# Retention and a swish layer on one core: first weights by half rows, ups in pairs of column groups, no copy of chunk 3's scores

## The chip, the cores and the metric

The kernel runs on one core of one Trainium2 chip. The metric is device time in microseconds (us): the median of three runs before the change is 311.66 us (311.6 to 312.2). The engines are named as the profile names them: PE (TensorE; PEld is its weight load), DVE (VectorE), ACT (ScalarE), POOL (GpSimd) and SP (SyncE, which here only issues DMAs).

## The reference

Eight batches with eight heads of 576 positions and 64 columns go through retention (scores times a decay that depends on the head and the distance, causal, without a softmax). The heads' outputs side by side are the 512 columns of 4608 tokens, and these go through a layer with a swish between its two products:

```python
scores = scale * np.matmul(q, k.transpose(0, 1, 3, 2))
gamma = 1.0 - 2.0 ** (-5.0 - np.arange(H, dtype=np.float32))
rel = pos[:, None] - pos[None, :]
Dmat = np.where(rel >= 0, gamma[:, None, None] ** rel[None, :, :], 0.0)
attn = np.matmul(scores * Dmat[None, :, :, :], v)
x = attn.transpose(0, 2, 1, 3).reshape(B * S, H * D)      # 4608 x 512
h = x @ w_in                                              # w_in 512 x 2048
g = h * (1.0 / (1.0 + np.exp(-beta * h)))                 # beta: 2048
out = g @ w_out                                           # w_out 2048 x 512
```

Inputs and output are float32.

## The kernel before

**Tiling.** The first 512 positions of each batch are a block of four chunks of 128; the last 64 of two batches make a tail chunk, and four tail chunks are the ninth block. Chunks are numbered in the order in which they are worked, so block 0 has chunks 0 to 3 and block 1 chunks 4 to 7. The decay is a factor on q (`gq`) and one on v (`gv`), so what stays of it in the scores is a mask of zeros and ones.

**Retention of one chunk i.** `pre` makes kn (k as bf16) and vn (v times its factor) on POOL. `t_k` turns kn on PE into a PSUM tile T, and ACT copies it to kT; `t_q` does the same for q, for half of the heads at a time. `a_sc` makes the scores of the eight heads (8 matmuls into two PSUM banks, even heads and odd heads) and DVE multiplies each bank with the mask into R. `a_O` multiplies R with vn (8 matmuls into a bank O), `a_cross` adds what the state of the earlier chunks gives (4 matmuls), and `a_x` copies O to xT, the transposed input of the layer. `a_st` adds the chunk to the state (4 matmuls), and ACT copies it to sbd (or end) in two pieces. In block 0 `a_cross` comes ahead of `a_O`, in block 1 behind it.

**The layer of one block m.** `up` makes one of 16 column groups of h: 4 matmuls (ko 0 to 3, one for each 128 rows of w_in) of 512 columns, and one ACT activation to gT. `down` is a quarter of the sum for one of four output tiles (4 matmuls); after a tile's last quarter DVE copies it to ot, and SP issues its store.

**Weights.** w_in is loaded in pieces of columns, four of 256 and two of 512, each with one DMA for all four row groups, into four staging tiles of 512 columns; `cast_w_in` casts each row group to bf16 on DVE or POOL. w_out comes in four groups of four column groups through the same four staging buffers, so each of its loads waits for the casts of the w_in tile whose buffer it takes; `cast_w_out` scales three on DVE and one on ACT.

**Order.** Nothing is scheduled by a planner: each engine's instructions stand in the order in which the program emits them, and each engine works its own in that order. Up to line 502 the order is written out by hand. Then `fill`, a list of ups and downs, is emitted one by one, and each step of `streams` is emitted ahead of the first fill entry whose number is not below the step's number. d0 is the number of block 0's first down (16), u1 that of block 1's first up (d0 + 16). Block 0's downs go by quarters for tiles 0 to 2 (d0 to d0 + 11), then tile 3 (d0 + 12 to d0 + 15).

**PSUM.** The eight banks are shared by tag: `mm` has three (ups, downs, warm-up matmuls, the second half of t_q, the scores of chunk 3), `O` two (O, T, and the scores of odd chunks from 5 on), `sc` two (other scores, T of chunks 6 and 7), `st` one. An instruction that opens a tile waits until the last reader of the bank's former tile is done.

**Lines.** L81 load_q, L94 load_kv, L178 load_w_in, L186 cast_w_in, L190 load_w_out, L198 and L200 cast_w_out, L208 warm_up, L247 qs, L255 vn, L273 kn, L297 and L303 transposes, L298 and L304 their copies, L323 scores, L330 the copy of chunk 3's odd scores, L333 the mask product, L351 the cross product, L366 O, L380, L381 and L384 xT, L396 and L401 the state, L413 and L415 up, L426 and L433 down, L436 the store.

Of the kernel before, what the change touches and what calls it, by code (L numbers as in the profile page):

```python
# [11 lines left out]
F32 = mybir.dt.float32  # L12
BF16 = mybir.dt.bfloat16
ACT = mybir.ActivationFunctionType
ALU = mybir.AluOpType
# [4 lines left out]
def kernel(  # L20
# [110 lines left out]
    for h in range(H):  # L131
# [13 lines left out]
    nc.gpsimd.memset(causal[:], 1.0)  # L145
    nc.gpsimd.affine_select(out=causal[:], in_=causal[:], pattern=[[1, CB], [CB, PC]], compare_op=ALU.is_ge,
                            fill=0.0, base=0, channel_multiplier=-1)
    causal4 = consts.tile([P, HP, P], BF16, name="causal4")
    nc.gpsimd.tensor_copy(causal4[:], causal[:].unsqueeze(1).to_broadcast([P, HP, P]))

    causal2 = consts.tile([P, P], BF16, name="causal2")

    NS = 3
# [10 lines left out]
    tiny = consts.tile([P, FO], F32, name="tiny")  # L164
    WG = 4

    pieces = [(f, 256) for f in range(0, 1024, 256)] + [(f, 512) for f in range(1024, d_ff, 512)]
    NP = len(pieces)
    w_in_r = moe_w_in.rearrange("(ko ki) f -> ki ko f", ki=P)
    w_out_r = moe_w_out.rearrange("(fo fi) n -> fi fo n", fi=P)  # L170
# [2 lines left out]
    def load_w_in(g):  # L173
        f0, fn = pieces[g]
        if f0 % 512 == 0:
            whole[0] = stage.tile([P, KO, 512], F32, name="wt", tag="wt", bufs=4)
        t = whole[0][:, :, f0 % 512:f0 % 512 + fn]
        nc.sync.dma_start(t, w_in_r[:, :, f0:f0 + fn])  # L178
        wts[g] = t

    def cast_w_in(g, kos=range(KO)):
        t = wts[g]
        f0, fn = pieces[g]
        for ko in kos:
            on_pool = ko == KO - 1 or g < 4 and ko > 1
            (nc.gpsimd if on_pool else nc.vector).tensor_copy(w_in_sb[:, ko, f0:f0 + fn], t[:, ko])  # L186

    def load_w_out(g):
        t = stage.tile([P, KO, d_model], F32, name="wt", tag="wt", bufs=4)
# [15 lines left out]
    def warm_up(n, cols=256):  # L205
        ph = psum.tile([P, MB], F32, name="ph", tag="mm", bufs=3)
        for _ in range(n):
            nc.tensor.matmul(ph[:, :cols], warm[:, :P], warm[:, :cols], start=True, stop=True,  # L208
                             skip_group_check=True)
# [41 lines left out]
    def pre(i, js=(0, 1)):  # L251

        b, c = seq[i]
        if 0 not in js:
            nc.gpsimd.tensor_tensor(live[i]["vn"][:], kv_tiles.pop(i)[:, 1], gains(gv, c), ALU.mult)  # L255
            return
        vn = sb.tile([P, H, D], BF16, name="vn", tag="vn", bufs=6)
        if b is None:
            t = tail_tiles.pop(c)
            qk = sb.tile([P, 2, H, D], BF16, name="kn", tag="kn", bufs=4)  # L260
            qkT = sb.tile([P, 2, HP, P], BF16, name="kT", tag="kT", bufs=4)
            nc.gpsimd.tensor_tensor(qk[:, 0], t[:, 0], gains(gq, CB), ALU.mult)
            nc.gpsimd.tensor_copy(qk[:, 1], t[:, 1])
            nc.gpsimd.tensor_tensor(vn[:], t[:, 2], gains(gv, CB), ALU.mult)
            live[i] = dict(qk=qk, qkT=qkT, kT=qkT[:, 1], vn=vn)
            return
        if c % 2 == 0:
            pair[b, c // 2] = (sb.tile([P, 2, H, D], BF16, name="kn", tag="kn", bufs=4),
                               sb.tile([P, 2, HP, P], BF16, name="kT", tag="kT", bufs=4))
        t = kv_tiles[i]  # L270
        kn, kT = pair[b, c // 2]
        live[i] = dict(kn=kn[:, c % 2], kT=kT[:, c % 2], vn=vn)
        nc.gpsimd.tensor_copy(kn[:, c % 2], t[:, 0])  # L273
        if 1 in js:
            pre(i, (1,))
# [24 lines left out]
    def t_k(i):  # L300
        T = psum.tile([P, HP, P], BF16, name="T", tag="sc" if i in (CB + 2, CB + 3) else "O", bufs=2)
        for p in range(HP):
            nc.tensor.transpose(T[:, p, :], heads(live[i]["kn"], p), ident[:])  # L303
        nc.scalar.copy(live[i]["kT"], T[:])  # L304

    def q_cols(i, r, p):

# [5 lines left out]
    def a_sc(i):  # L313
        L = live[i]
        L["R"] = R = sb.tile([P, 2, HP, P], BF16, name="R", tag="R", bufs=4)

        tag = "mm" if i == CB - 1 else "O" if i >= E and (i - E) % 2 else "sc"
        sc = [psum.tile([P, HP, P], F32, name="sc", tag=tag, bufs=3 if tag == "mm" else 2) for _ in range(2)]
        for p in range(HP):
            for j in range(2):  # L320
                r = slice(j * D, (j + 1) * D)
                rhs, view = q_cols(i, r, p)
                nc.tensor.matmul(view(sc[j][:, p, :]), L["kT"][r, p, :], rhs, start=True, stop=True,  # L323
                                 skip_group_check=True)
        mask = causal if seq[i][0] is not None else causal2
        m_b = mask[:].unsqueeze(1).to_broadcast([P, HP, P])
        if i == CB - 1:

            half = sb.tile([P, HP, P], BF16, name="half", tag="half", bufs=1)
            nc.scalar.copy(half[:], sc[1][:])  # L330
            sc[1] = half
        for j in range(2):
            nc.vector.tensor_tensor(R[:, j], sc[j][:], causal4[:] if i == CB - 1 else m_b, ALU.mult)  # L333

    def a_cross(i, first):

# [17 lines left out]
    def a_O(i):  # L354

        b, c = seq[i]
        L = live[i]

        early = i < E
        if not early:  # L360
            tag = "sc" if b is not None and b >= QB and c > 1 else "O"
            L["O"] = psum.tile([P, HP, P], F32, name="O", tag=tag, bufs=2)
        O, R, vn = L["O"], L["R"], L["vn"]
        crossed = b is None or c > 0
        for j, p in [(n // HP, n % HP) if early else (n % 2, n // 2) for n in range(H)]:
            nc.tensor.matmul(O[j * D:(j + 1) * D, p, :], vn[:, 2 * p + j, :], R[:, j, p, :],  # L366
                             start=p == 0 and not (early and crossed), stop=early or not crossed,
                             skip_group_check=True)
        if early:
            a_x(i)  # L370

    def a_x(i):
        b, c = seq[i]
        O = live[i]["O"]
        if b is None:
            x = xt(B)[:, :, c, :]
        else:
            x, O = xt(b)[:, :, :, c * PC:(c + 1) * PC], O.rearrange("k p (i s) -> k p i s", i=CB)
        if i == CB - 1:
            nc.vector.tensor_copy(x[:, :2], O[:, :2])  # L380
            nc.scalar.copy(x[:, 2:], O[:, 2:])  # L381
        else:
            on_act = i < E or i % 2 == 0 if i < 2 * E else b is not None and c == 1
            (nc.scalar.copy if on_act else nc.vector.tensor_copy)(x, O[:])  # L384

    def a_st(i):
# [19 lines left out]
    def up(m, fo, c0=0, cn=CB):  # L406
        if m not in gts:
            gts[m] = sb.tile([P, FO, CB, P], BF16, name="gT", tag="gT", bufs=2)
        w = slice(c0 * PC, (c0 + cn) * PC)
        ph = psum.tile([P, CB, P], F32, name="ph", tag="mm", bufs=3)  # L410
        ph = ph.rearrange("f i s -> f (i s)")[:, :cn * P].rearrange("f (i s) -> f i s", i=CB)
        for ko in range(KO):
            nc.tensor.matmul(ph, w_in_sb[:, ko, fo * P:(fo + 1) * P], xts[m][:, ko, :, w],  # L413
                             start=(ko == 0), stop=(ko == KO - 1))
        nc.scalar.activation(gts[m][:, fo, :, w], ph, ACT.Silu, scale=beta_sb[:, fo:fo + 1])  # L415

    pos_, ots = {}, {}

# [34 lines left out]
    def F(f, *a):  # L453
        return lambda: f(*a)
# [17 lines left out]
    warm_up(1, 128)  # L472
    a_cross(0, True)
    a_O(0)
    a_sc(1)
    a_cross(1, True)
    pre(2, (0,))
# [3 lines left out]
    pre(3, (0,))  # L481
    a_sc(2)
    t_k(3)
    warm_up(1, 128)
    a_cross(2, True)
    a_sc(3)
    pre(2, (1,))
    a_st(2)
    a_O(2)
    pre(3, (1,))  # L490
    warm_up(2, 128)
    a_cross(3, True)
    a_O(3)
    cast_w_in(0)
    a_st(3)
    cast_w_in(1)
    nc.vector.reciprocal(rbeta_sb[:], beta_sb[:])

# [2 lines left out]
                            fill=0.0, base=0, channel_multiplier=-1)  # L501
    nc.gpsimd.memset(causal2[:TL, TL:], 0.0)

    fill = [F(up, 0, fo) for fo in range(FO)]
    d0 = len(fill)
    fill += [F(down, 0, ms, f0) for f0 in range(0, FO, 4) for ms in range(3)]
    fill += [F(down, 0, 3, f0) for f0 in range(0, FO, 4)]
# [13 lines left out]
    def second(i):  # L521
        for f in (a_O, lambda j: a_cross(j, False), a_x):
# [1 line left out]
            f(i + 1)  # L524
        a_st(i + 1)

    streams = [[(0, F(load_w_out, 0)), (1.1, F(cast_w_in, 2)), (3.1, F(cast_w_in, 3)), (3.2, F(load_w_out, 1)),
                (6.1, F(cast_w_in, 4)), (6.2, F(load_w_out, 2)), (10.1, F(cast_w_in, 5)), (10.2, F(load_w_out, 3))],
               [(d0 - 4 + 3.3 * g, F(cast_w_out, g)) for g in range(WG)],
               [(10.3, F(load_q, 1))] + [(10.3, F(load_kv, CB + n, (j,))) for n, j in keys_first],  # L530
               [(10.4, F(load_q, 2))] + [(10.4, F(load_kv, 2 * CB + n)) for n in range(2)],
               [(d0 + 8.6, F(load_kv, 2 * CB + 2)), (d0 + 10.1, F(load_kv, 2 * CB + 3))],
               [(d0 + 7, F(pre_q, 1, n)) for n in range(4)] + [(d0 + 10.6, F(t_q, 1, 0)), (d0 + 12.6, F(t_q, 1, 1))],
               [(d0 + 8, F(pre, 4, (0,))), (d0 + 8, F(pre, 5, (0,))), (d0 + 9, F(pre, 4, (1,))), (d0 + 9, F(pre, 5, (1,))),
                (d0 + 12.7, F(t_k, 4)), (d0 + 12.8, F(t_k, 5)), (d0 + 13.8, F(a_sc, 4)), (d0 + 13.81, F(a_sc, 5)),
                (d0 + 14.8, F(a_st, 4)), (d0 + 15.9, F(second, 4))],
               [(d0 + 10, F(pre, 6, (0,))), (d0 + 10, F(pre, 7, (0,))), (d0 + 12, F(pre, 6, (1,))), (d0 + 12, F(pre, 7, (1,))),
                (d0 + 15.8, F(t_k, 6)), (d0 + 15.91, F(t_k, 7)), (u1 + 1.8, F(a_sc, 6)), (u1 + 1.81, F(a_sc, 7)),
                (u1 + 2.8, F(a_st, 6)), (u1 + 8.8, F(second, 6))]]
# [81 lines left out]
```

## Time and profile before

| | us |
|---|---|
| median of three runs | 311.66 |
| the profiled execution | 311.92 |
| its span (first to last instruction) | 310.1 |
| PE busy | 298.5 (96%) |
| ACT busy | 143.0 (46%) |
| DVE busy | 106.9 (34%) |
| POOL busy | 96.0 (31%) |
| first up of block 0 | 19.48 |
| first down of block 0 | 34.28 |
| first up of block 1 | 52.22 |
| last matmul ends | 306.83 |

A row of the timeline gives start, length, engine, line, operation, the tile written and the tile read, and the count; in brackets stands how long the engine had been idle and what ended that. A row of the chain of waits gives start, length and the work that the end of the program goes back to. The granted clock of PE is 0.998 of the full one.

### The profile page before, as it was taken

Reading aid. Unit: us, or ns where it says so; the run is one execution under the profiler, and the core shown is the slowest. Engines: PE = TensorE matmul, PEld = TensorE weight load, DVE = VectorE, ACT = ScalarE, POOL = GpSimd, SP = SyncE. Lnnn points to the kernel's source line nnn. Section 1 sums busy time; section 2 is a strip of 40 time slices with the busy share of each in tenths; the row PEclk is TensorE's granted clock in tenths of the full one; section 3 lists DMA queues with packets and bytes.
Section 4 is the critical chain, followed back from the end, with each engine's and each line's share of the span. In section 5 each row is a group of like instructions: output and inputs, shape, how many; then the busy total and the mean of one; then the engine's idle time right before and its main releaser. Section 6 shows DMA issues by size and latency. Waiting matters only on the chain.

```text
span 310.1 us, 5363 instructions
## 1 busy us (share of the span) xinstructions
PE 298.5 (96%) x2144; PEld 157.8 (51%) x2177; DVE 106.9 (34%) x191; ACT 143.0 (46%) x256; POOL 96.0 (31%) x131
## 2 busy tenths in 40 slices
PE   7789999999999999999999999999999999999995
PEld 5544456775544454454554545455545444444444
DVE  7554476342531342434430434043405420010012
ACT  5567626995138412560186117711673037207700
POOL 4663026846524282254308031902420000000000
PEclk9999999999999999999999999999999999999999
DMA  8999999998989999999897697968852110031011
GB/s 207 221 355 387 380 232 273 233 257 179 202 197 162 224 189 235 218 212 198 133 234 107 136 205 207 201 115 192 196 76 37 68 70 0 17 88 34 0 70 68
DMA packets 123897, 52.79 MB, mean 170 GB/s; under 512 B 105680, under 2 KB 116320, under 8 KB 123872
## 3 DMA queue, kind: packets, MB, share of 16 engines
q1 hardware_dynamic: 98496, 46.15, 61.5%
q10 hardware_dynamic: 25376, 6.30, 13.6%
q8 instruction: 17, 0.28, 0.4%
q14 instruction: 8, 0.07, 0.1%
HBM read 36.71 MB, written 9.44 MB: 149 GB/s over the span
## 4 chain that ended last, share of the span: by engine, by line
PE 85%; DMA 6%; SPq 5%; DVE 1%; issue 1%; ACT 1%; POOL 1%; POOLq 0%
PE po L426 40%; PE ph L413 35%; DMA wt<-in_moe_w_in_dram 4%; SPq L94 3%; PE O L366 3%; PE sc L323 3%; DMA qn<-in_q_dram 2%; PE O L351 2%; PE st L396 2%; SPq L178 1%; POOL qs L247 1%; PE T L297 1%; PE T L303 1%; ACT gT L415 0%; DVE xT L384 0%
## 5 line engine op out<-in xcount | busy, mean ns | idle before, releaser
L415 ACT ACTIVATE gT<-ph,beta_sb 128x512 bf16<-128x512 f32 (+1 forms) x154 | 99.2, 659 | 86.3 <-PE ph L413 83.4
L413 PE MATMUL ph<-xT,w_in_sb 128*128 128x512 bf16 (+1 forms) x600 | 129.3, 365 | 3.2 <-DVE w_in_sb L186 0.9
L426 PE MATMUL po<-w_out_sb,gT 128*128 128x512 bf16 (+2 forms) x591 | 126.7, 368 | 1.1 <-issue 0.3
L413 PEld LDWEIGHTS <-w_in_sb 128*128 128x128 bf16 x616 | 58.7, 98 | 65.0 <-DVE w_in_sb L186 2.3
L426 PEld LDWEIGHTS <-gT 128*128 128x128 bf16 x608 | 57.1, 98 | 62.5
L333 DVE TENSOR_TENSOR R<-sc,causal 128x512 bf16<-128x512 f32 x71 | 44.3, 684 | 68.9 <-PE sc L323 68.9
L433 DVE COPY ot<-po 128x512 f32<-128x512 f32 (+2 forms) x38 | 25.0, 662 | 92.1 <-PE po L426 92.0
L255 POOL TENSOR_TENSOR vn<-kvn,gv 128x512 bf16<-128x512 f32 x32 | 33.4, 1042 | 22.8 <-DMA kvn<-in_v_dram 11.5
L247 POOL TENSOR_TENSOR qs<-qn,gq 128x512 bf16<-128x512 f32 x24 | 24.3, 1042 | 33.2 <-DMA qn<-in_q_dram 33.2
L273 POOL CAST kn<-kvn 128x512 bf16<-128x512 f32 x32 | 19.6, 612 | 47.7 <-DMA kvn<-in_k_dram 47.3
L401 ACT CAST sbd<-st 64x256 bf16<-64x256 f32 x48 | 17.4, 362 | 15.0 <-PE st L396 14.3
L384 DVE CAST xT<-O 128x512 bf16<-128x512 f32 x24 | 15.8, 688 | 19.6 <-PE O L366 9.6
L384 ACT CAST xT<-O 128x512 bf16<-128x512 f32 x11 | 6.4, 586 | 32.2 <-PE O L351 25.2
L396 PE MATMUL st<-vn,kn 128*128 128x128 bf16 x128 | 12.4, 219 | 0.2 <-POOL vn L255 0.2
L396 PEld LDWEIGHTS <-kn 128*128 128x128 bf16 x128 | 9.3, 98 | 5.0 <-issue 0.2
L366 PE MATMUL O<-R,vn 128*64 128x128 bf16 x288 | 10.7, 221 | 0.0
L323 PE MATMUL sc<-qT,kT 64*128 64x128 bf16 x256 | 10.3, 217 | 0.4 <-ACT kT L304 0.2
L366 PEld LDWEIGHTS <-vn 128*64 128x64 bf16 x288 | 8.5, 110 | 4.1 <-issue 3.6
L323 PEld LDWEIGHTS <-kT 64*128 64x128 bf16 x288 | 8.1, 94 | 3.8 <-ACT kT L304 1.5
L304 ACT COPY kT<-T 128x512 bf16<-128x512 bf16 x12 | 6.9, 586 | 4.8 <-PE T L303 4.8
L208 PE MATMUL ph<-warm 128*128 128x128 f32 (+1 forms) x24 | 7.0, 429 | 1.2 <-DVE warm L119 1.2
L186 DVE CAST w_in_sb<-wt 128x256 bf16<-128x256 f32 (+1 forms) x14 | 6.0, 476 | 5.2 <-DMA wt<-in_moe_w_in_dram 5.2
(56 smaller groups left out, 90.2 us busy)
## 6 DMA issues: line engine op xcount, KB each, us to landing
qn<-in_q_dram SPq DMA_DIRECT2D x16, 512.0 KB, 5.8
kvn<-in_k_dram SPq DMA_DIRECT2D x32, 256.0 KB, 5.9
kvn<-in_v_dram SPq DMA_DIRECT2D x32, 256.0 KB, 5.6
out_dram<-ot SPq DMA_DIRECT2D x31, 256.0 KB, 2.7
wt<-in_moe_w_out_dram SPq DMA_DIRECT2D x4, 1024.0 KB, 9.5
wt<-in_moe_w_in_dram SPq DMA_DIRECT2D x4, 512.0 KB, 7.5
wt<-in_moe_w_in_dram SPq DMA_DIRECT2D x2, 1024.0 KB, 11.8
out_dram<-ot SPq DMA_DIRECT2D x9, 128.0 KB, 2.4
```

The lines of the kernel that those rows point to most:

```text
L247: e.tensor_tensor(batch[b]["qs"][:, cs, hs], q_tiles[b][:, hs, cs].rearrange("p h i d -> p i h d"), gq[:, cs, hs].unsqueeze(3).to_broadcas ...
L255: nc.gpsimd.tensor_tensor(live[i]["vn"][:], kv_tiles.pop(i)[:, 1], gains(gv, c), ALU.mult)
L273: nc.gpsimd.tensor_copy(kn[:, c % 2], t[:, 0])
L323: nc.tensor.matmul(view(sc[j][:, p, :]), L["kT"][r, p, :], rhs, start=True, stop=True, skip_group_check=True)
L333: nc.vector.tensor_tensor(R[:, j], sc[j][:], causal4[:] if i == CB - 1 else m_b, ALU.mult)
L366: nc.tensor.matmul(O[j * D:(j + 1) * D, p, :], vn[:, 2 * p + j, :], R[:, j, p, :], start=p == 0 and not (early and crossed), stop=early or ...
L384: (nc.scalar.copy if on_act else nc.vector.tensor_copy)(x, O[:])
L396: nc.tensor.matmul(st[:, p, :], heads(L["kn"], p), heads(L["vn"], p), start=(c == 0 and p == 0), stop=True, skip_group_check=True)
L413: nc.tensor.matmul(ph, w_in_sb[:, ko, fo * P:(fo + 1) * P], xts[m][:, ko, :, w], start=(ko == 0), stop=(ko == KO - 1))
L415: nc.scalar.activation(gts[m][:, fo, :, w], ph, ACT.Silu, scale=beta_sb[:, fo:fo + 1])
L426: nc.tensor.matmul(po[:, :nn], gT[:, fo, ms, :], w_out_sb[:, fo, n0:n0 + nn], start=(fo == 0), stop=(fo == FO - 1))
L433: nc.vector.tensor_copy(ot, po[:, :nn])
```

## The change

- w_in is loaded in six pieces of 256 columns and one of 512, each by two DMAs, one for its first two row groups and one for the other two.
- `cast_w_in` gives even row groups to DVE and odd ones to POOL; of the first piece group 0 goes to POOL, 1 to ACT, 2 to DVE, 3 to POOL.
- Block 0's ups go in pairs of column groups: the matmuls of ko 0 and 1 for both, then those of ko 2 and 3 for both, each group's activation behind its own.
- Chunk 3's odd scores are multiplied with the mask straight from PSUM; the copy `half` and the widened mask `causal4` are gone.
- `a_x` of chunks 0 to 3 is called by itself, for chunk 1 behind the transposes of chunk 3's keys. xT of chunks 3, 5 and 7 is copied by halves, by DVE and ACT; of chunks 4 and 6 by ACT. kT of chunks 5 and 7 is copied by DVE.
- `a_st(3)` stands between the two halves of the first pair. Casts, loads of w_out and block 1's transposes, scores and chunk 4's state have other numbers in `streams`.

```diff
-    causal4 = consts.tile([P, HP, P], BF16, name="causal4")
-    nc.gpsimd.tensor_copy(causal4[:], causal[:].unsqueeze(1).to_broadcast([P, HP, P]))
...
-    pieces = [(f, 256) for f in range(0, 1024, 256)] + [(f, 512) for f in range(1024, d_ff, 512)]
+    pieces = [(f, 256) for f in range(0, 1536, 256)] + [(f, 512) for f in range(1536, d_ff, 512)]
...
         t = whole[0][:, :, f0 % 512:f0 % 512 + fn]
-        nc.sync.dma_start(t, w_in_r[:, :, f0:f0 + fn])
+        for u in range(2):
+            w = slice(u * KO // 2, (u + 1) * KO // 2)
+            nc.sync.dma_start(t[:, w], w_in_r[:, w, f0:f0 + fn])
...
         for ko in kos:
-            on_pool = ko == KO - 1 or g < 4 and ko > 1
-            (nc.gpsimd if on_pool else nc.vector).tensor_copy(w_in_sb[:, ko, f0:f0 + fn], t[:, ko])
+            if g == 0 and ko == 1:
+                nc.scalar.copy(w_in_sb[:, ko, f0:f0 + fn], t[:, ko])
+            else:
+                on_pool = ko == 0 if g == 0 and ko < 2 else ko % 2
+                (nc.gpsimd if on_pool else nc.vector).tensor_copy(w_in_sb[:, ko, f0:f0 + fn], t[:, ko])
...
-        nc.scalar.copy(live[i]["kT"], T[:])
+        (nc.vector.tensor_copy if i > CB and i % 2 else nc.scalar.copy)(live[i]["kT"], T[:])
...
-        if i == CB - 1:
-
-            half = sb.tile([P, HP, P], BF16, name="half", tag="half", bufs=1)
-            nc.scalar.copy(half[:], sc[1][:])
-            sc[1] = half
         for j in range(2):
-            nc.vector.tensor_tensor(R[:, j], sc[j][:], causal4[:] if i == CB - 1 else m_b, ALU.mult)
+            nc.vector.tensor_tensor(R[:, j], sc[j][:], m_b, ALU.mult)
...
-        if early:
-            a_x(i)
...
-        if i == CB - 1:
+        if i < 2 * CB and i % 2 and i != 1:
             nc.vector.tensor_copy(x[:, :2], O[:, :2])
             nc.scalar.copy(x[:, 2:], O[:, 2:])
         else:
-            on_act = i < E or i % 2 == 0 if i < 2 * E else b is not None and c == 1
+            on_act = i < 2 * E or b is not None and c == 1
             (nc.scalar.copy if on_act else nc.vector.tensor_copy)(x, O[:])
...
+    def up_half(m, fo, u):
+
+        if m not in gts:
+            gts[m] = sb.tile([P, FO, CB, P], BF16, name="gT", tag="gT", bufs=2)
+        for f in (fo, fo + 1):
+            if u == 0:
+                phs[f] = psum.tile([P, MB], F32, name="ph", tag="mm", bufs=3)
+            for ko in range(u * KO // 2, (u + 1) * KO // 2):
+                nc.tensor.matmul(phs[f][:], w_in_sb[:, ko, f * P:(f + 1) * P], xts[m][:, ko],
+                                 start=(ko == 0), stop=(ko == KO - 1))
+            if u:
+                nc.scalar.activation(gts[m][:, f], phs[f][:], ACT.Silu, scale=beta_sb[:, f:f + 1])
...
     a_O(0)
+    a_x(0)
...
     t_k(3)
+    a_x(1)
     warm_up(1, 128)
...
     a_O(2)
+    a_x(2)
...
     a_O(3)
+    a_x(3)
     cast_w_in(0)
-    a_st(3)
     cast_w_in(1)
...
-    fill = [F(up, 0, fo) for fo in range(FO)]
+    fill = [F(up_half, 0, fo, u) for fo in range(0, FO, 2) for u in range(2)]
...
-    streams = [[(0, F(load_w_out, 0)), (1.1, F(cast_w_in, 2)), (3.1, F(cast_w_in, 3)), (3.2, F(load_w_out, 1)),
-                (6.1, F(cast_w_in, 4)), (6.2, F(load_w_out, 2)), (10.1, F(cast_w_in, 5)), (10.2, F(load_w_out, 3))],
+    streams = [[(0, F(load_w_out, 0)), (0.05, F(a_st, 3)), (0.1, F(cast_w_in, 2)), (2.1, F(cast_w_in, 3)), (2.2, F(load_w_out, 1)),
+                (4.1, F(cast_w_in, 4)), (6.1, F(cast_w_in, 5)), (6.2, F(load_w_out, 2)), (8.1, F(cast_w_in, 6)),
+                (8.2, F(load_w_out, 3))],
                [(d0 - 4 + 3.3 * g, F(cast_w_out, g)) for g in range(WG)],
...
-               [(d0 + 7, F(pre_q, 1, n)) for n in range(4)] + [(d0 + 10.6, F(t_q, 1, 0)), (d0 + 12.6, F(t_q, 1, 1))],
+               [(d0 + 7, F(pre_q, 1, n)) for n in range(4)] + [(d0 + 12, F(t_q, 1, 0)), (d0 + 13, F(t_q, 1, 1))],
...
-                (d0 + 12.7, F(t_k, 4)), (d0 + 12.8, F(t_k, 5)), (d0 + 13.8, F(a_sc, 4)), (d0 + 13.81, F(a_sc, 5)),
-                (d0 + 14.8, F(a_st, 4)), (d0 + 15.9, F(second, 4))],
+                (d0 + 14, F(t_k, 4)), (d0 + 14.1, F(t_k, 5)), (d0 + 15, F(a_sc, 4)), (d0 + 15.01, F(a_sc, 5)),
+                (d0 + 15.7, F(a_st, 4)), (d0 + 15.9, F(second, 4))],
                [(d0 + 10, F(pre, 6, (0,))), (d0 + 10, F(pre, 7, (0,))), (d0 + 12, F(pre, 6, (1,))), (d0 + 12, F(pre, 7, (1,))),
                 (d0 + 15.8, F(t_k, 6)), (d0 + 15.91, F(t_k, 7)), (u1 + 1.8, F(a_sc, 6)), (u1 + 1.81, F(a_sc, 7)),
                 (u1 + 2.8, F(a_st, 6)), (u1 + 8.8, F(second, 6))]]
```

More of the change, by code (lines that the diff above doesn't have):

```diff
@@ L415, in up @@
         nc.scalar.activation(gts[m][:, fo, :, w], ph, ACT.Silu, scale=beta_sb[:, fo:fo + 1])
+    phs = {}
+    def up_half(m, fo, u):
[9 more added lines that the diff above has]
+                nc.scalar.activation(gts[m][:, f], phs[f][:], ACT.Silu, scale=beta_sb[:, f:f + 1])
     pos_, ots = {}, {}
```

## The prediction

> **What bounds the kernel now.** I read the page's busy shares first: TensorE (PE) is the bound.
>
> ```profile
> PE 298.5 (96%) x2144; PEld 157.8 (51%) x2177; DVE 106.9 (34%) x191; ACT 143.0 (46%) x256; POOL 96.0 (31%) x131
> PE   7789999999999999999999999999999999999995
> ```
>
> Only 11.6 us of the 310.1 us span have no matmul. The answer by stages (length, then busy PE) says where: 4.71 before 20.0, 0.49 to 34.3, 0.48 from 47.7 to 52.2, 0.28 to 59.4, 2.36 in the 247.5 us after that, 3.2 behind the last matmul. So the edits can win about 1 us at the start and about 1 us of idle spread over blocks 0 and 1; whatever idle they add on PE is lost, because nothing later has room to take it back.
>
> The timeline of the start shows what the first up waits for:
>
> ```profile
> 18.59 0.42 DVE L380 CAST xT<-O 128x256 bf16<-128x256 f32 x1 [1.04 <-PE O L366]
> 18.88 0.80 POOL L186 CAST w_in_sb<-wt 128x256 bf16<-128x256 f32 x2 [1.75 <-DMA wt<-in_moe_w_in_dram]
> 18.93 0.90 DVE L186 CAST w_in_sb<-wt 128x256 bf16<-128x256 f32 x2
> 19.05 0.37 ACT L381 CAST xT<-O 128x256 bf16<-128x256 f32 x1 [0.71 <-DVE xT L380]
> 19.48 0.10 PEld L413 LDWEIGHTS <-w_in_sb 128*128 128x128 bf16 x1 [0.79 <-DVE w_in_sb L186]
> ```
>
> Piece 0 has landed at 18.88; ACT's half of chunk 3's xT starts only after DVE's (19.01). The same timeline asked for 26 to 50 us, and for DVE and ACT alone, gives the end of block 0's ups and the start of block 1's attention:
>
> ```profile
> 28.77 1.51 DVE L186 CAST w_in_sb<-wt 128x512 bf16<-128x512 f32 x3 [1.20 <-DMA wt<-in_moe_w_in_dram]
> 31.53 0.72 ACT L198 ACTIVATE w_out_sb<-wt,rbeta_sb 128x512 bf16<-128x512 f32 x1
> 31.55 1.28 DVE L200 TENSOR_SCALAR w_out_sb<-wt,rbeta_sb 128x512 bf16<-128x512 f32 x3 [1.27 <-DMA wt<-in_moe_w_out_dram]
> 32.16 1.98 ACT L415 ACTIVATE gT<-ph,beta_sb 128x512 bf16<-128x512 f32 x3
> ...
> 48.07 2.48 DVE L333 TENSOR_TENSOR R<-sc,causal 128x512 bf16<-128x512 f32 x4 [0.94 <-PE sc L323]
> 50.47 0.68 DVE L433 COPY ot<-po 128x512 f32<-128x512 f32 x1
> ```
>
> w_out's first group lands at 31.5, and ACT's cast of it stands in ACT's queue ahead of three activations. DVE makes four R in a row, then copies the last output. The chain of waits has the same stage on PE:
>
> ```profile
> 34.28 8.63 PE po L426 x40
> ...
> 47.70 0.55 PE sc L323 x16
> ...
> 50.54 0.57 PE O L366 x16
> 51.10 0.34 PE O L351 x4
> ...
> 51.47 0.70 DVE xT L384
> ...
> 52.22 1.05 PE ph L413 x8
> ```
>
> Marks to follow: downs of block 0 begin at 34.28, scores of chunks 4 and 5 at 47.70, ups of block 1 at 52.22.
>
> **Part 1, chunk 3.** Without the half copy (0.58 of ACT) the state copies (16.97 to 17.73, for which the cross product at 17.78 waits) end near 17.36; behind the warm-up matmuls the cross product starts near 17.5, and O of chunk 3 is done 0.27 earlier: DVE's xT half at 18.32 to 18.74, ACT's at 18.78 to 19.15. The second mask product is 0.69 rather than 0.41, but O needs it late: nothing. kT of chunk 3 now comes before chunk 1's xT on ACT, worth about 0.15, contained in the 0.27. causal4 (POOL, 0.61 at 3.08) goes where POOL idles 2.33: nothing; without that idle, 0.61.
>
> **Part 2, first up.** Landings (18.88, 20.35, 21.85, 23.34, then 26.06, 28.77, 31.5) give 1.49 per 512 KB piece 256 columns wide and 2.71 per 1 MB piece 512 wide. The first half should land 0.75 before 18.88, near 18.1. But its second row group (ko 1) is cast by ACT, which does it after its xT half: 19.15 + 0.37 (the ACT row of that size) = 19.5. So PE does one matmul early and the rest from 19.55, not from 19.88. Then 63 of 64 matmuls at 0.2158 (40 po in 8.63) and the moved a_st(3) (0.22; it stood in a gap before) end at 33.4.
>
> The pairs add waits. A pair holds two of the three mm buffers, so the second group of the next pair needs the first activation of this one: done 1.295 (six matmuls) + 0.20 (last matmul to ACT: a matmul starts at 20.11, group 1's last ends six later at 21.41, its activation starts at 21.61) + 0.69 + 0.05 (56.02 to 56.07, where PE waits for ACT in the chain) = 2.24 into the pair, wanted at 1.73 + 0.43 = 2.16. That is 0.08 a pair, 0.5 in all, and 0.35 more after the first, where activation 0 stands behind the end copies of a_st(3) (0.74, now emitted behind the first cast): 34.2.
>
> The other casts cost nothing: they alternate between DVE (0.35) and POOL (0.46), and pieces land every 1.5 us where PE takes 1.73 for a pair. The last piece gives POOL two casts of 0.87 instead of one, done near 30.0 and wanted near 30.6; uncovered that would be 0.9. SP's eight more issues (0.56 each, by the rows from 13.28) stretch its w_in queue, which ends at 18.84, to 23 at most; w_out's loads stand behind them, but DMA has w_in bytes to move until 29, so nothing.
>
> **Part 3, the w_out cast as a gate.** The cast stays at position 12 of the fill list. Two more pieces are 256 wide: 2 x 1.49 - 2.71 = 0.27 later, and eight more DMAs cost from nothing (the engines stay busy across the pieces, at about 385 GB/s) to 0.15 each (a tenth of a piece); I take 0.02, near the lower end, since no gap between pieces shows. So w_out lands at 31.5 + 0.27 + 0.16 = 31.9 (31.5 to 33). Behind ACT's cast (0.63 to the next start, 31.53 to 32.16) group 12's activation ends at 33.22; only then can group 15 take its buffer and start (33.27), with six matmuls left of the pair: 33.27 + 1.295 = 34.56. Downs begin 0.28 later than now (bounds -0.1 with w_out at 31.5, +1.35 at 33), and the front's gain is gone. What follows on the queue, 0.4 later as well: w_out's other groups are cast 1.2 to 1.4 ahead of use now; block 1's qs is made by 44.4 instead of 43.95 and turned at 44.9. Nothing for both, 0.3 at the upper bound.
>
> The Trainium skill ("DMA: Bandwidth & Descriptors", Anatomy of one DMA) gives each DMA a fixed 2.0 us besides its bytes. As a queue's price, eight more would be 16 us and the time 327; the 1.49 spacing shows that this part overlaps here.
>
> **Part 4, block 1's attention.** The new positions put 15 instead of 13 downs ahead of chunk 4's scores, and the last down between those of chunk 4 and of chunk 5. Scores 4 start at 34.56 + 15 x 0.863 + 0.90 (T of q) + 0.44 (T of k) = 48.85. Count from there (t). kT of chunk 5 is now DVE's: its transposes start at t - 0.22 and take 0.40, the copy some 0.38 (an estimate from DVE's 0.69 for 1024 columns of the same type at 46.43), so it ends at 0.59 and the first R, which could start at 0.43 (14.27 to 14.70 for chunk 2), starts 0.13 later at 0.56. Four R take 2.48 now; but the last output copy comes to stand between the pairs, since its down is emitted before scores 5: R, R, ot, R, R at 0.62 each and 0.07 of tail, third R done at 3.10, fourth at 3.71. O of chunks 4 and 5 take the O buffers that hold chunk 5's scores, so they wait for exactly these two R. PE meanwhile has 0.28 + 0.86 + 0.28 + 0.22 + 0.22 = 1.86: idle from 1.86 to 3.15, and after O 4 (0.28) to 3.76. O 5 and its cross product end at 4.26; DVE's half of xT runs 4.44 to 4.86, ACT's 4.90 to 5.27; with a_st(5) and T(7) beside them, the ups run as if from 5.08 (ko 2 at 5.32, less two matmuls). So the stretch has 5.08 - 3.08 (its matmul work, the scores and O pieces of the chain and one down) = 2.0 of idle. Now it is 52.22 - 47.70 - 3.96 (the same work and one more down) = 0.56. The loss is 1.4: 1.0 if PE's issue takes 0.4 less than I count on either side of R, 1.8 if ACT's activations, behind its xT half and the state copies, hold the first ups for 0.4. kT of chunk 7, and of 9 and 11 later, goes to an idle DVE (1.47 idle before 53.63): nothing either way, 0.2 at most if it meets an R.
>
> The split of xT saves less than it looks: DVE's half ends 0.27 sooner, but ACT's starts after it, 0.14 later than the whole copy's end. The row is ACT's 0.71 of idle at 19.05. The Trainium skill ("PSUM — Partial Sum Buffer", PSUM bank collisions) wants two engines kept apart on one bank even for reads; the row agrees; halves at once would give 0.3 back, and the time would be 313.0.
>
> Chunk 6 and 7: xT is ready at 59.40 and PE has an up beside it: nothing. After 59.4 all follows PE rigidly.
>
> **Sum.** 0.28 + 1.4 = +1.7 on the profiled 311.92 us (span 310.1 and 1.8 around it), 313.6; the median is 0.26 lower: 311.66 + 1.7 = 313.3.
>
> **Rivals.** Front wins (not slower): if the ups run from 18.8 and group 15 is not held by ACT, 64 x 0.2158 + 0.22 end at 32.8, 1.45 before now; against the 1.4 of part 4 this leaves 311.6. For it: PE's 0.62 of idle at 19.48. Against: ACT's row at 31.53. It decides where ups end by 33.5 (34.28 - 1.4 + 0.6); with the lower 1.0 for part 4 it ends at 311.2. Chance 0.10 (310.9 to 312.3).
> Many DMAs: at 0.1 to 0.15 each w_out lands at 32.6 to 33, downs begin 0.95 to 1.35 later, and with 1.4 that is 314.2. For it: SP already takes 0.54 to 1.15 to issue a piece. Against: pieces land 1.49 apart, so issue is not the bound. Chance 0.15 (313.9 to 314.9).
> Absorbed: part 4 costs 1.0 and the 0.6 that PE waits at 165.24 for ACT behind POOL's qs vanishes: 311.66 + 0.28 + 1.0 - 0.6 = 312.3. Against: that wait starts from an output of block 3, so it moves with PE. Chance 0.12 (312.1 to 312.7).
> Halves that don't work as halves, a cast waiting for the whole piece, change nothing: ko 1 comes at 19.5 either way.
>
> **Numbers.** The forecast holds 0.63 (312.7 to 313.9). Range 312.2 to 314.4: it leaves out Front wins and a part of Many DMAs, some 0.2. This kernel's measurement can tell 0.2%, 0.6 us, from no change: the bounds are 311.0 and 312.3. Faster 0.06, same 0.08, slower 0.86.
>
> **What would show it.** Part 1 and 2: xT halves near 18.3 and 18.8, steady ups from 19.5. Part 3: ACT's first w_out cast near 31.9, PE idle about half a us before group 15, downs from 34.5. Part 4: an ot copy between two R pairs on DVE near 50.5, over 1 us of idle on PE before O of chunk 4 near 52.0, ups of block 1 from 53.9. Downs before 33.5, or O right behind T(6), would prove it wrong.

## The result, and the profile after

The changed kernel takes 313.57 us (median of four runs, 313.24 to 313.88) against 311.63 for the one before beside it: 1.9 us slower by these medians. The ratio of the two is put at 1.0053 with a 95% interval of 1.0037 to 1.0068, which is 1.7 us, from 1.2 to 2.1. The prediction said 313.3 (+1.7), from 312.2 to 314.4. The profiled execution took 313.81 us with a span of 312.1.

The page's busy shares and PE's slices, of the changed kernel:

```profile
PE 301.2 (97%) x2177; PEld 157.8 (51%) x2177; DVE 106.5 (34%) x194; ACT 140.9 (45%) x254; POOL 98.3 (31%) x134
PE   7789998999999999999999999999999999999995
```

The shares tell nothing of a loss: ACT and DVE have less to do, and PE's busy time rose partly because this trace holds all 2177 matmuls where the one before holds 2144. The marks on the way do tell. The start of block 0's ups in the changed kernel's timeline:

```profile
18.09 0.40 POOL L188 CAST w_in_sb<-wt 128x256 bf16<-128x256 f32 x1 [0.78 <-DMA wt<-in_moe_w_in_dram]
18.55 0.42 DVE L375 CAST xT<-O 128x256 bf16<-128x256 f32 x1 [0.66 <-PE O L363]
19.01 0.37 ACT L376 CAST xT<-O 128x256 bf16<-128x256 f32 x1 [0.71 <-DVE xT L375]
19.13 0.38 PE L422 MATMUL ph<-xT,w_in_sb 128*128 128x512 bf16 x1 [0.63 <-DVE xT L375]
19.28 0.41 ACT L185 CAST w_in_sb<-wt 128x256 bf16<-128x256 f32 x1
19.74 0.82 PE L422 MATMUL ph<-xT,w_in_sb 128*128 128x512 bf16 x3 [0.24 <-ACT w_in_sb L185]
```

The half piece is there at 18.09 and one matmul goes early; the next waits until ACT, behind its half of xT, has cast the second row group. ACT at the end of block 0's ups, and DVE in block 1's attention, in the same kernel's timeline:

```profile
30.60 1.26 ACT L425 ACTIVATE gT<-ph,beta_sb 128x512 bf16<-128x512 f32 x2 [0.54 <-PE ph L422]
31.82 0.72 ACT L200 ACTIVATE w_out_sb<-wt,rbeta_sb 128x512 bf16<-128x512 f32 x1
32.44 1.25 ACT L425 ACTIVATE gT<-ph,beta_sb 128x512 bf16<-128x512 f32 x2
...
48.95 0.42 DVE L306 COPY kT<-T 128x512 bf16<-128x512 bf16 x1 [1.48 <-PE T L305]
49.29 1.28 DVE L330 TENSOR_TENSOR R<-sc,causal 128x512 bf16<-128x512 f32 x2
50.48 0.68 DVE L443 COPY ot<-po 128x512 f32<-128x512 f32 x1
51.08 1.28 DVE L330 TENSOR_TENSOR R<-sc,causal 128x512 bf16<-128x512 f32 x2
```

The output copy stands between the two pairs of R. Its chain of waits (start, length, work) says what that does to the order of PE's work:

```profile
34.62 10.36 PE po L436 x48
...
48.95 0.42 DVE kT L306
49.37 1.20 DVE R L330 x2
50.56 0.60 DVE ot L443
51.16 1.21 DVE R L330 x2
...
52.41 0.41 PE O L363 x8
52.83 0.34 PE O L348 x4
...
53.20 0.44 DVE xT L375
...
53.68 0.39 PE ph L408 x2
...
54.89 0.55 PE sc L325 x16
...
60.32 0.44 DVE xT L375
...
60.78 0.37 ACT xT L376
61.15 0.26 ACT end L396
...
61.42 0.37 ACT end L396
...
61.81 0.48 ACT gT L410
...
62.34 1.91 PE ph L408 x16
64.25 0.45 PE T L299 x8
```

From 48.95 to 52.37 the chain lies on DVE, where before it lay on PE from the scores of chunk 4 to O. The lower part is new too: DVE's half of chunk 7's xT, ACT's half, ACT's two copies of the state to `end`, and then the activation that frees the buffer for which PE waits at 62.34. In the chain of the kernel before, the ups ran on at 59.44 as soon as DVE's whole copy was done:

```profile
53.27 0.55 PE sc L323 x16
...
58.70 0.70 DVE xT L384
...
59.44 2.79 PE ph L413 x24
62.24 0.45 PE T L297 x8
```

Three stages share the loss. "w_out" is when the first group has landed (DVE's first cast of it), the next column where block 0's downs begin; the last two are distances, from there to the scores of chunk 6 and on to the transposes of block 2's q. The lower rows are experiments told next, one profiled execution each. The marks of PE are the chain's; the timeline has the first down 0.16 earlier (34.12 before, 34.46 in the changed kernel).

| kernel | w_out | first down | to scores of 6 | on to T of q |
|---|---|---|---|---|
| before | 31.55 | 34.28 | 18.99 | 8.97 |
| changed | 31.83 | 34.62 | 20.27 | 9.36 |
| e1_positions_only | 31.50 | 34.23 | 20.36 | 8.97 |
| e2_old_positions | 31.93 | 34.72 | 18.89 | 9.35 |
| e3_chunk7_whole | 32.22 | 35.01 | 20.27 | 8.97 |
| e4_no_pairs | 31.68 | 34.04 | 20.38 | 9.36 |
| e5_gate_open | 31.89 | 34.63 | 20.27 | 9.35 |
| e7_scores_together | 31.98 | 34.77 | 19.68 | 9.35 |
| b2_qs_on_pool | 31.79 | 33.83 | 18.89 | 8.98 |

So the change loses 0.34 in the front (0.35 to 0.73 in the four other executions with its pairs, most where w_out landed last), 1.28 in block 1's attention and 0.39 behind chunk 7. That is 2.01, and the span grew by 2.0.

### The profile page after: what moved, and what is told of

It is laid out like the page before. It is cut to its first block, busy times and chain, and to the rows that moved or that the text cites. A ratio compares the mean times of both kernels' runs of the same rounds, so it can differ in the third digit from the quotient of the medians.

```text
span 312.1 us, 5409 instructions
## 1 busy us (share of the span) xinstructions
PE 301.2 (97%) x2177; PEld 157.8 (51%) x2177; DVE 106.5 (34%) x194; ACT 140.9 (45%) x254; POOL 98.3 (31%) x134
## 4 chain that ended last, share of the span: by engine, by line
PE 86%; SPq 4%; DMA 4%; DVE 2%; ACT 1%; POOL 1%; issue 1%; ACTq 0%; POOLq 0%
PE po L436 40%; PE ph L408 32%; PE ph L422 4%; SPq L94 3%; PE O L363 3%; PE sc L325 2%; DMA wt<-in_moe_w_in_dram 2%; DMA qn<-in_q_dram 2%; PE O L348 2%; PE st L391 2%; DVE R L330 1%; SPq L177 1%; POOL qs L249 1%; ACT gT L410 1%; PE T L299 1%
## 5 line engine op out<-in xcount | busy, mean ns | idle before, releaser
L436 PE MATMUL po<-w_out_sb,gT 128*128 128x512 bf16 (+2 forms) x608 | 129.0, 368 | 0.0
L410 ACT ACTIVATE gT<-ph,beta_sb 128x512 bf16<-128x512 f32 (+1 forms) x138 | 88.3, 656 | 82.2 <-PE ph L408 81.2
L408 PE MATMUL ph<-xT,w_in_sb 128*128 128x512 bf16 (+1 forms) x552 | 116.3, 364 | 1.2 <-ACT gT L410 1.1
L330 DVE TENSOR_TENSOR R<-sc,causal 128x512 bf16<-128x512 f32 x72 | 45.0, 683 | 66.5 <-PE sc L325 66.5
L257 POOL TENSOR_TENSOR vn<-kvn,gv 128x512 bf16<-128x512 f32 x32 | 33.3, 1042 | 23.5 <-PE O L363 11.0
L379 DVE CAST xT<-O 128x512 bf16<-128x512 f32 x22 | 14.5, 688 | 16.6 <-PE O L363 9.6
L422 PE MATMUL ph<-xT,w_in_sb 128*128 128x512 bf16 x64 | 14.9, 378 | 1.1 <-DVE xT L375 0.6
L425 ACT ACTIVATE gT<-ph,beta_sb 128x512 bf16<-128x512 f32 x16 | 10.1, 682 | 3.2 <-PE ph L422 3.2
```

What stands on the lines that cost most here:

```text
L330: nc.vector.tensor_tensor(R[:, j], sc[j][:], m_b, ALU.mult)
L422: nc.tensor.matmul(phs[f][:], w_in_sb[:, ko, f * P:(f + 1) * P], xts[m][:, ko], start=(ko == 0), stop=(ko == KO - 1))
L436: nc.tensor.matmul(po[:, :nn], gT[:, fo, ms, :], w_out_sb[:, fo, n0:n0 + nn], start=(fo == 0), stop=(fo == FO - 1))
```

## The experiments

Each time is the median of 6 to 12 executions, against 16 to 23 of the kernel before that ran beside them; each mark on the way comes from one profiled execution.

**The order in block 1, alone.** Kernel before, with the new numbers:

```diff
-(d0 + 10.6, F(t_q, 1, 0)), (d0 + 12.6, F(t_q, 1, 1))
+(d0 + 12, F(t_q, 1, 0)), (d0 + 13, F(t_q, 1, 1))
...
-(d0 + 12.7, F(t_k, 4)), (d0 + 12.8, F(t_k, 5)), (d0 + 13.8, F(a_sc, 4)), (d0 + 13.81, F(a_sc, 5)), (d0 + 14.8, F(a_st, 4))
+(d0 + 14, F(t_k, 4)), (d0 + 14.1, F(t_k, 5)), (d0 + 15, F(a_sc, 4)), (d0 + 15.01, F(a_sc, 5)), (d0 + 15.7, F(a_st, 4))
```

> The kernel before with only the changed kernel's new numbers for block 1's transposes of q and k, scores of chunks 4 and 5 and state of chunk 4. My theory (the order in block 1 costs the time): block 0's downs begin where they did (34.3), the last output copy comes between the R pairs, PE idles over 1 us ahead of O of chunk 4, block 1's ups begin near 53.6 instead of 52.2, time 313.0 (+1.4). Rival (the loss comes with the front or with kT and xT on other engines): ups of block 1 by 52.6, time 311.9.

313.21 us against 311.88, ratio 1.0046 (1.0030 to 1.0062). Its chain of waits:

```profile
34.23 8.63 PE po L426 x40
...
48.89 1.28 DVE R L333 x2
50.17 0.60 DVE ot L433
50.77 1.21 DVE R L333 x2
...
52.02 0.41 PE O L366 x8
...
52.80 0.70 DVE xT L384
...
53.55 0.50 PE ph L413 x3
```

Downs begin as early as before, and block 1's ups at 53.55: the same R, ot, R as in the changed kernel, without any other part of the change. The table gives 1.37 for the order alone.

**The old order in the changed kernel** (the same lines the other way).

> The changed kernel with the old numbers for block 1's transposes, scores and state of chunk 4. My theory: downs begin at 34.6 as in the changed kernel, scores of chunk 4 near 48.0, ups of block 1 near 52.5, and what stays is the front's 0.3 and 0.4 behind chunk 7's xT: 312.3. Rival (the loss is not in the order): 313.4, nothing won.

312.08 against 311.88, ratio 1.0011 (1.0000 to 1.0022). Scores of chunk 6 come 18.89 after the first down instead of 20.27. Both ways round, the order is worth 1.4. What stays is the front (0.44 in this execution) and chunk 7 (0.38), less 0.10 that the halves of chunk 5's xT win. DVE's copies of kT win nothing: O of chunk 4 comes 2.83 behind the scores of chunk 4 here, and 2.84 in the kernel before.

**Chunk 7's xT whole on DVE.**

```diff
-if i < 2 * CB and i % 2 and i != 1:
+if i in (CB - 1, CB + 1):
...
-on_act = i < 2 * E or b is not None and c == 1
+on_act = i < 2 * E and i != 2 * CB - 1 or b is not None and c == 1
```

> The changed kernel with xT of chunk 7 copied whole by DVE, as before. Theory (the ACT half stands ahead of the end copies and the activation that frees an up's buffer, PE waits 0.6 for that activation at 62.3): the wait goes, the stage behind comes 0.4 earlier, 313.2. Rival (the wait belongs to ACT's end copies alone and stays, or another takes its place): 313.6.

313.19 against 311.88, ratio 1.0048 (1.0029 to 1.0066). The chain of waits:

```profile
60.70 0.70 DVE xT L379
...
61.45 1.05 PE ph L408 x8
```

No ACT stands in it any more, and the last column falls to 8.97, that of the kernel before. So the trace shows the 0.39; the time can't, since its interval and that of the changed kernel overlap. In this execution w_out landed late, at 32.2, and ACT's timeline shows what the prediction called the gate:

```profile
32.21 0.72 ACT L200 ACTIVATE w_out_sb<-wt,rbeta_sb 128x512 bf16<-128x512 f32 x1 [0.36 <-DMA wt<-in_moe_w_out_dram]
32.83 1.25 ACT L425 ACTIVATE gT<-ph,beta_sb 128x512 bf16<-128x512 f32 x2
```

ACT is idle, waiting for the load with two activations behind it.

**Ups one at a time.**

```diff
-fill = [F(up_half, 0, fo, u) for fo in range(0, FO, 2) for u in range(2)]
+fill = [F(up, 0, fo) for fo in range(FO)]
```

> The changed kernel with block 0's ups one group at a time (four row groups in a row), everything else of the change kept. If the three buffers cost 0.08 a pair and the first pair's wait 0.35 to 0.6, and the w_out cast on ACT gates group 15 (cast at 31.8, activation of group 12 done at 33.1): downs begin at 34.05, 313.0. If that cast gates nothing: downs begin at 33.55, 312.5. If the pairs cost nothing: downs begin at 34.6 and 313.6.

313.51 against 311.88, ratio 1.0058 (1.0038 to 1.0078). Downs begin at 34.04, as the two costs together had it, 0.58 before the changed kernel's. The time (313.0 expected) doesn't show it within its interval.

**Without the gate**, first with the pairs, then without them. The line says which casts of w_out go to ACT, the others go to DVE:

```diff
-if i == KO - 1:
+if i == KO - 1 and g > 0:
```

> The changed kernel, but DVE makes the fourth cast of w_out's first group too, so ACT's queue holds no wait for that load among block 0's activations. Gate theory (the prediction): group 15 no longer waits for the load, downs begin by the pairs' own waits alone, 34.4 wherever w_out lands; time 313.3 to 313.5. Rival (the pairs' waits alone bound it, the gate was never shut): downs at 34.6, nothing changes, 313.6.

313.67 against 311.80, ratio 1.0067 (1.0047 to 1.0086); downs at 34.63. Here the rival was nearer: the pairs' waits alone end the ups at 34.6. In the four executions with pairs and gate (changed, e2, e3, e7) downs begin 2.79 behind w_out's landing each time, so the gate does set the end, but only by what it adds to the pairs' own end: some 0.03 in the changed kernel's profile (34.62 against e5's 34.63, whose second pair was let go 0.04 later, at 22.37 instead of 22.33) and 0.4 where w_out landed at 32.22.

> The changed kernel with both: ups one group at a time and DVE's cast of the first w_out group. If pairs and gate are the front's two costs, PE runs from the first up to the first down without a wait after the start: downs at 33.6 (34.04 without the gate's change), ups of block 1 near 52.8, 313.0. If something else holds the front (arrival of w_in), downs stay near 34.0 and time near 313.5.

313.50 against 311.80, ratio 1.0057 (1.0039 to 1.0076). Downs begin near 33.8, 0.8 before the changed kernel's, and yet block 1's ups begin at 53.42 (52.8 expected), 0.26 earlier only. The time is the one that the rival gave, but not for the rival's reason. The timeline of PE shows a wait that had not been expected:

```profile
45.02 1.02 PE L436 MATMUL po<-w_out_sb,gT 128*128 128x512 bf16 x4 [0.38 <-DVE ot L443]
```

The three output tiles hold all three mm buffers until DVE copies them, and DVE's copies stand behind the products of block 1's q, whose second load landed at 43.1. Between the first transposes of q and the next down, 1.00 passes here (44.02 to 45.02) and 0.44 in the changed kernel (44.82 to 45.26), so this takes back 0.56. A faster front runs into the arrival of q.

**Both scores ahead of the last down** (in the changed kernel, `a_sc(5)` at d0 + 15).

> The changed kernel with the scores of chunk 5 put right behind those of chunk 4, ahead of the last down, so that DVE makes four R in a row and the output copy comes after them. Theory (half of block 1's loss is the output copy between the R pairs, the rest is that too little PE work is left behind the scores): O of chunk 4 waits 0.6 less, its second wait stays small, block 1's ups begin 0.6 earlier, 313.0. Rival one (the output copy only fills time in which DVE would wait for chunk 5's scores): no change, 313.6. Rival two (all of the loss is that copy): 312.3.

313.19 against 311.80, ratio 1.0047 (1.0030 to 1.0065). The distance falls from 20.27 to 19.68, the 0.6 of one output copy; the time can't tell it from the changed kernel's. The other 0.8 of the order is that only one down, not two, lies between the scores and O while DVE makes four R. In PE's rows the scores of chunk 4 start 14.39 behind the first down here and 13.52 with the old order (e2), one down later; from there to the scores of chunk 6 both take about 5.4, though PE has a down of 0.86 less to do in it here.

**All three mended.** No pairs, no gate, old order, chunk 7 whole:

> The changed kernel without pairs, with DVE's cast of the first w_out group, the old numbers for block 1's attention and chunk 7's xT whole on DVE. If the three costs add up: downs at 33.6, ups of block 1 at 51.3, 310.6. Rival (block 1's q and k land no earlier, so PE then waits for qT, kT or an output buffer in block 0's last downs): downs at 33.6 but ups of block 1 near 52, 311.3.

311.78 against 311.80, ratio 0.9998 (0.9985 to 1.0012). The sum of the parts would have been 310.6; the rival had the mechanism, though its 311.3 was too low as well. Downs begin at 33.8, but PE waits 0.69 at 45.31 for an output buffer, and the scores of chunk 6 come at 53.56, 0.3 later than in the kernel before. Two more edits follow, one on what is late next (the engine of the products `pre_q`) and one on the first up:

```diff
-e = nc.vector
+e = nc.gpsimd if (b, n) == (1, 2) else nc.vector
```

> b1_all_mended with one of the four products of block 1's q (the third, the first that needs q's second load) on POOL instead of DVE. In b1 PE waits 0.7 at 45.3 for an output buffer, whose copy stands in DVE's queue behind the two products that wait for q's second load at 43.4. Theory (the arrival of q has become the bound, through DVE's queue): the copies begin 0.6 earlier, PE's wait nearly goes, ups of block 1 at 51.7, time 311.2. Rival (POOL's product delays kn of chunks 4 and 5 or PE waits next for qT): ups at 52.3 as in b1, 311.8.

311.24 against 311.71, ratio 0.9998 (0.9979 to 1.0017). PE's wait for an output buffer is gone and block 1's ups begin at 51.51, 0.8 earlier than in b1; the interval is too wide to tell the time from that of before.

```diff
-if g == 0 and ko == 1:
-    nc.scalar.copy(w_in_sb[:, ko, f0:f0 + fn], t[:, ko])
-else:
-    on_pool = ko == 0 if g == 0 and ko < 2 else ko % 2
+on_pool = ko != 2 if g == 0 else ko % 2
```

> b2_qs_on_pool with both casts of the first half piece on POOL, so that the second row group is not behind ACT's half of chunk 3's xT. Theory for the front (ACT's place for that cast costs PE 0.4 to 0.5 at 19.7): PE runs on from the first up, downs at 33.2. For the end: if q's arrival bounds, the 0.4 comes back as a wait ahead of block 1's transposes of q and ups stay near 51.7, 311.2; if not, 51.3 and 310.8.

311.05 against 311.71, ratio 0.9980 (0.9967 to 0.9994): the one version of the ten here that is clear of the kernel before, by 0.6 us (0.2 to 1.0). PE in the timeline of the start, then the chain of waits:

```profile
19.15 1.02 PE L405 MATMUL ph<-xT,w_in_sb 128*128 128x512 bf16 x4 [0.63 <-POOL w_in_sb L185]
```

```profile
31.16 11.99 DMA qn<-in_q_dram
...
43.78 0.69 DVE ot L440
...
44.51 1.02 PE po L433 x4
```

The first up runs without the stop and downs begin near 33.3, 0.5 earlier than in b2, but a wait at 44.51 takes all of it back: block 1's ups begin at 51.57, as in b2 (51.51). The start of block 1 is now bound by the load of q. What b3 has over b2 in time is not shown to come from its edit.

## Why the prediction was right, point by point

**Part 1, chunk 3.** Expected 0.27 earlier; DVE's half began at 18.55 instead of 18.59, in an execution whose keys of chunk 3 came 0.15 later (cast at 13.90, not 13.75). So about 0.2, and it bought only one matmul. The prediction let the state copies end near 17.36; they ran from 16.93, since they also wait for PE's state matmuls (16.50 to 16.90).

**Part 2, first up and pairs.** The stop behind ACT's cast was foreseen at 19.55 and measured at 19.74. b3 shows that ACT's place for this cast was its cause. Pairs follow each other every 1.80 in ACT's rows (23.39, 25.19, 26.99, 28.79), 0.07 over PE's 1.73, where 0.08 was worked out. The second pair is held to 22.33 by the first activation behind the end copies; the prediction's terms give 22.14, earlier by the 0.19 that the start is late. The pairs' path was set at 34.2 and is 34.46 in the timeline of e5 (34.63 in its chain); most of that is this 0.19.

**Part 3, the gate.** w_out landed at 31.83 (31.9 expected) and downs began at 34.46 in the timeline, 34.62 in the chain (34.56 expected). The sum mixes the two: its 34.56 is counted as the timeline counts, and was set against the chain's 34.28. Against the timeline's 34.12 its 0.28 would have been 0.44; measured is 0.34 either way. The mechanism is there, but its weight was mis-sized: the prediction let it decide alone, while the pairs' path ended within 0.03 of it. That the front came out close to the forecast although the gate hardly held it is in part luck.

**Many DMAs.** From the changed kernel's rows at 18.09 and 26.33 (the first and the twelfth half piece of 256 columns) a half lands every 0.749; before, a half's share was 0.743. A further DMA on this queue cost 0.006, not 0.02 and not 0.1. The 2.0 us that the prediction takes from the Trainium skill ("DMA: Bandwidth & Descriptors", Anatomy of one DMA) is given there for the path by way of GpSimd; these loads were issued by SP, and the measured 0.006 decides. No execution with halves had w_out before 31.68 or after 32.3.

**Part 4, block 1.** Expected 1.4; measured 1.28 to the scores of chunk 6. Scores of chunk 4 came at 48.84 (48.85 expected), then R, R, ot, R, R, and O of chunks 4 and 5 at 2.98 and 3.57 behind them where 3.15 and 3.76 were worked out. Most of the difference is DVE's copy of kT, for which 0.13 had been counted: it began 0.1 earlier and cost nothing, since in e1, where ACT makes it, the two O come at 2.97 and 3.57. Block 1's first up came at 53.68, 53.9 was expected. e1 and e2 show that the order did it, e7 that the output copy is 0.6 of it. DVE's copy of kT took 0.42, set at 0.38. The 0.1 by which the changed kernel is ahead of e1 in this stage (20.27, not 20.36) is that of the halves of chunk 5's xT.

**Chunk 7, the step that failed.** It was set at nothing, since xT came in time and an up stood beside it. The whole path was not followed: ACT's half stands in ACT's queue ahead of the end copies and the activations, and PE is one buffer from waiting for these. That is 0.39, shown by e3. In the profile, front and block 1 lose 1.62 where 1.68 was forecast, and chunk 7 makes it 2.01; the times can't tell 1.7 from 2.0. That the halves are taken one after the other held: ACT's half began after DVE's each time in the changed kernel (19.01 behind 18.97, 53.65 behind 53.62, 60.78 behind 60.75), as the Trainium skill asks for one bank ("PSUM — Partial Sum Buffer", PSUM bank collisions). No run here shows what halves at once would do.

**Rivals.** Front wins was wrong on both its conditions, ups ended at 34.6. Absorbed had one thing right: PE's 0.6 at 165.24 is not fixed, and the prediction's "nothing later has room" was wrong there. The wait is in the traces of before and after (0.60 at 165.24, 0.65 at 167.18) and not in those of e1 and e2, whose longest wait on PE behind 100 us is 0.2. In e1 block 2's scores come 1.33 later than before, but the scores behind that wait only 0.45 later, and its span is 310.6 for that reason; in the changed kernel 2.01 becomes 1.94. What sets the length of this wait was not followed, so a span or a time of a single execution says less here than a mark ahead of it. Of the 2.36 of idle that the prediction counted behind 59.4, part is matmuls that its trace lacks: in the changed kernel's trace, which has all of them, 0.98 is left between the same two marks of time.

## What to carry to other kernels

When a step is moved to a later place in a hand-made order, count what the other engines then have queued between its parts: one output copy of 0.6 between two pairs of products, and one cover of 0.86 less on PE, cost 1.4 us here, while DVE was busy for a third of the time. A copy that is split between two engines to shorten it is on the queue of both: follow the second engine's queue down to the next buffer that it must free. And before a start is sped up, ask which load the end of that stage will meet: here the front could give 0.8, and without moving a product out of DVE's queue only 0.26 of it arrived at block 1's ups.

## What the runs showed of the hardware

Two casts side by side on DVE and POOL don't share evenly. In the changed kernel DVE's cast of 256 columns takes 0.29 where it starts first (20.31) and POOL's beside it 0.52; where POOL starts first (18.85) POOL takes 0.40 and DVE 0.50. POOL alone took 0.40 as well (18.09). So the one that started second took some 0.1 to 0.2 longer; 0.07 of DVE's 0.50 is overlap with its own copy before it.
